# Converting float64 weight words with a clamp, a Prelu and a shift

## The chip, the cores and the metric

One core of a Trainium2 chip runs the whole program. Five engines work beside each other, each with its own instruction queue in order: TensorE (PE in the profile; PEld is its weight load), VectorE (DVE), ScalarE (ACT), GpSimd (POOL) and SyncE (SP), which here issues every DMA. The metric is the device time of one execution in microseconds.

## The reference, cut to what matters

Causal attention over 4 batches, 12 heads, 448 positions and head dimension 64, then a two-layer network over the 1792 tokens (768 to 2048 to 768) with an ELU between the layers. The two weight matrices arrive as float64.

```python
scores = scale * np.matmul(q, k.transpose(0, 1, 3, 2))
scores = np.where(mask, -1000000000.0, scores)
attn = np.exp(scores - np.max(scores, axis=-1, keepdims=True))
attn = attn / (np.sum(attn, axis=-1, keepdims=True) + 1e-09)
x = np.matmul(attn, v)            # heads side by side: 1792 x 768
h = x @ w_in                      # 768 x 2048, float64
g = np.where(h > 0.0, h, np.exp(np.minimum(h, 0.0)) - 1.0)
out = g @ w_out                   # 2048 x 768, float64
```

## The kernel before

The 448 positions are cut into four groups of 112 (`NG`); a group holds its 112 positions of all four batches, so 448 columns of a matmul. For each group g the kernel runs the two layers (`emit_h`, 16 output blocks of 6 products each; `emit_o`, 6 output blocks of 16) and, woven in between, the attention of group g+1 (`attention`). The first group's attention (`first_pair`) stands ahead of all.

Most matmuls of the layers are made of three products of fp32r parts (`three`, L581 to L583): high weight by high activation, high by low, low by high. So each weight piece w is split: `wh` is its rounding to fp32r (L571), `wl` the rest, w - wh (L572, on VectorE or GpSimd). The first eight blocks of group 0 (`PLAIN`) use plain fp32 matmuls instead (L597) and need no split.

A weight piece is 128 x 768 or 128 x 512 words. There are 34: 16 of `w_in`, 18 of `w_out` (12 of 768 and 6 of 512 columns). In group 0 each is read as float64 (L542), converted to float32, and written to HBM (L562); groups 1 to 3 read the float32 copy (L565). The conversion in `weights` goes over the words as pairs of 32 bits, low and high, that lie alternately, so that the high words are read with a stride of 8 bytes:

- L545, ScalarE: the absolute value of the high word, read as a float, into w
- L546, VectorE: the minimum with `MOST`, times `REBIAS` = 2^-112, in place in w
- L549, VectorE: the sign bit of the high word, in place
- L552, VectorE: w shifted left by 3, or the sign
- L556, ScalarE: the low word times 2^-29, as an integer, in place
- L559, GpSimd: the integer sum of the two

The order on all engines is written out ahead of time by a planner (`Plan`). Each piece of work has one or more ways (engine, cost in us, instruction, and whether it occupies the port that VectorE and GpSimd share), what it reads and writes, and a due time. `run` simulates the engines with these costs, takes at each step the work that can start first, among near ties the one due first, and takes a second way only where the first would finish later. Work whose buffer is not yet free waits (`Ring`): `w` has 5 buffers, the group of float64 words and split weights (`w6`) 8, and the accumulator of a layer (`hp`) 3. A w buffer of group 0 is free when its write to HBM has landed and its split is made. What the planner wrote is then the fixed order of each engine's queue.

Of the kernel before, what the change touches and what calls it, by code (L numbers as in the profile page):

```python
# [11 lines left out]
U32 = mybir.dt.uint32  # L12
I32 = mybir.dt.int32
AF = mybir.ActivationFunctionType
ALU = mybir.AluOpType
# [8 lines left out]
MOST = struct.unpack("<f", struct.pack("<I", 0x47EFFFFF))[0]  # L24
REBIAS = 2.0 ** -112
# [43 lines left out]
class Plan:  # L69
# [4 lines left out]
    def __init__(self):  # L74
        self.works = []

    def add(self, ways, reads=(), writes=(), due=None, size=0.0, hold=()):


        if isinstance(ways, tuple):  # L80
            ways = [ways]
        full = lambda x: [(b, None) if isinstance(b, Buf) else b for b in x]
        reads, writes = full(reads), full(writes)
        w = Work(ways, size, due, reads, writes, hold)
        meet = lambda a, b: a is None or b is None or a == b
        for b, key in reads:
            w.preds |= {o for o, k, wr in b.uses if wr and meet(k, key)}
        for b, key in writes:
            w.preds |= {o for o, k, wr in b.uses if meet(k, key)}
        for b, key in reads:  # L90
            b.uses.append((w, key, False))
        for b, key in writes:
            b.uses.append((w, key, True))
        for b in w.bufs:
            b.left += 1
        for p in w.preds:
            p.succs.append(w)
        self.works.append(w)
        return w
# [87 lines left out]
def attention_moe_kernel(ctx, tc, qk, v, w_in, w_out, out):  # L187
    nc = tc.nc
# [5 lines left out]
    scale = 1.0 / math.sqrt(D)  # L194
# [10 lines left out]
        out=ident, in_=ident, pattern=[[-1, CP]], compare_op=ALU.not_equal,  # L205
# [5 lines left out]
        out=mask[:, S - CP:], in_=mask[:, S - CP:], pattern=[[-1, CP]], compare_op=ALU.is_ge,  # L211
# [3 lines left out]
    def f32(ap):  # L215
        return ap.bitcast(F32)
# [5 lines left out]
    plan = Plan()  # L222
# [10 lines left out]
    def new(tag, shape, dtype=F32, name=None):  # L233
        pool = ps if tag in ("hp", "p", "av") else sb
        ring = rings.setdefault(tag, Ring(BUFS[tag], in_order=tag != "p"))
        return ring.new(lambda: pool.tile(shape, dtype, tag=tag, name=name or tag, bufs=BUFS[tag]))
# [4 lines left out]
    def act(n, fn, more=0.05):  # L241
        return ("ACT", more + 0.84e-3 * n, fn, False)

    def dve(n, fn, rate=1.05e-3, more=0.08, port=False):
        return ("DVE", more + rate * n, fn, port)

    def pool(n, fn, rate=2.3e-3):
        return ("POOL", 0.1 + rate * n, fn, True)

    def dma(kb, rows, fn, reads, writes):  # L250
        plan.add(("SP", 0.35 + 0.5e-3 * rows, fn, False), reads, writes, size=kb / 260.0)
# [276 lines left out]
    def weights(g, key):  # L528
        if key[0] == "i":
            src, n = w_in[key[1]], KT  # L530
        else:
            f0, n = FG[key[2]]
            src = w_out[key[1], :, f0:f0 + n]
        size = n * P
        w = new("w", [P, KT, P])
        if g == 0:
            r = w64[key]
            name = "w32_" + "_".join(map(str, key))
            k = kept[key] = Buf(None, lambda: dram.tile([P, n, P], F32, name=name))
            low, high = (lambda: r()[:, :n, :, 0]), (lambda: r()[:, :n, :, 1])  # L540
            wf = lambda: w()[:, :n]
            dma(n * P, P, lambda: nc.sync.dma_start(  # L542
                out=r()[:, :n].rearrange("p k c w -> p k (c w)"), in_=src.bitcast(U32)
            ), [], [r])
            plan.add(act(size, lambda: nc.scalar.activation(wf(), f32(high()), AF.Abs)), [(r, 1)], [w])  # L545
            plan.add(dve(size, lambda: nc.vector.tensor_scalar(  # L546
                wf(), wf(), MOST, REBIAS, op0=ALU.min, op1=ALU.mult
            ), 0.55e-3, 0.06, True), [], [w])
            plan.add(dve(size, lambda: nc.vector.tensor_scalar(  # L549
                high(), high(), 0x80000000, None, op0=ALU.bitwise_and  # L550
            ), 0.55e-3, 0.06, True), [], [(r, 1)])
            plan.add(dve(size, lambda: nc.vector.scalar_tensor_tensor(  # L552
                out=wf().bitcast(U32), in0=wf().bitcast(U32), scalar=3, in1=high(),
                op0=ALU.logical_shift_left, op1=ALU.bitwise_or,
            ), port=True), [(r, 1)], [w])
            plan.add(act(size, lambda: nc.scalar.activation(  # L556
                low().bitcast(I32), low(), AF.Copy, scale=2.0 ** -29
            )), [], [(r, 0)])
            plan.add(pool(size, lambda: nc.gpsimd.tensor_tensor(  # L559
                out=wf().bitcast(I32), in0=wf().bitcast(I32), in1=low().bitcast(I32), op=ALU.add  # L560
            )), [(r, 0)], [w])
            dma(n * 64, P, lambda: nc.sync.dma_start(out=k(), in_=wf()), [w], [k])  # L562
        else:
            k = kept[key]
            dma(n * 64, P, lambda: nc.sync.dma_start(out=w()[:, :n], in_=k()), [k], [w])  # L565
        if g == 0 and key[0] == "i" and key[1] < PLAIN:
            wt[(g, *key)] = (w,)
            return
        t = whl[key] if g == 0 else new("w6", [P, 2, KT, P], F32R, "whl")
        wh, wl = (lambda: t()[:, 0]), (lambda: t()[:, 1])  # L570
        plan.add(act(size, lambda: nc.scalar.activation(wh()[:, :n], w()[:, :n], AF.Copy)), [w], [(t, 0)])  # L571
        sub = lambda eng: lambda: eng.tensor_tensor(  # L572
            out=wl()[:, :n], in0=w()[:, :n], in1=f32(wh()[:, :n]), op=ALU.subtract
        )
        plan.add([dve(size, sub(nc.vector), port=True), pool(size, sub(nc.gpsimd))], [w, (t, 0)], [(t, 1)])
        wt[(g, *key)] = t, wh, wl
# [12 lines left out]
    def emit_h(g, f, k, due):  # L589
        if k == 0:  # L590
            weights(g, ("i", f))
            st["h"] = new("hp", [P, S], name="hp")
        hp = st["h"]
        w, x = wt[g, "i", f], xt[g, k]
        if len(w) == 1:
            x = xf[k]
            pe(ONE, lambda: nc.tensor.matmul(hp(), w[0]()[:, k], x(), start=k == 0, stop=k == KT - 1), [*w, x], [hp], due)  # L597
        else:
            pe(THREE, lambda: three(hp, w, k, x, k == 0, k == KT - 1), [w[0], *x], [hp], due)
        if k < KT - 1:  # L600
            return
        m = new("m", [P, S])
        gh, gl = new("gh", [P, S], F32R), new("gl", [P, S], F32R)
        plan.add(act(S, lambda: nc.scalar.activation(m(), hp(), AF.Relu, scale=-1.0)), [hp], [m])  # L604
        plan.add(act(S, lambda: nc.scalar.activation(m(), m(), AF.Exp, scale=-1.0)), [], [m])  # L605
        plan.add(dve(S, lambda: nc.vector.scalar_tensor_tensor(  # L606
            out=hp(), in0=m(), scalar=-1.0, in1=hp(), op0=ALU.add, op1=ALU.max
        )), [m], [hp])
        plan.add(act(S, lambda: nc.scalar.activation(gh(), hp(), AF.Copy)), [hp], [gh])
        plan.add(dve(S, lambda: nc.vector.tensor_tensor(  # L610
            out=gl(), in0=hp(), in1=f32(gh()), op=ALU.subtract
        )), [hp, gh], [gl])
        gt[f] = gh, gl

    def emit_o(g, e, f, due):
        x = f // FG[0][1]
        if f == FG[x][0]:
            weights(g, ("o", e, x))
        if f == 0:
            st["o"] = new("hp", [P, S], name="op")  # L620
        op = st["o"]
        w, gg = wt[g, "o", e, x], gt[f]
        pe(THREE, lambda: three(op, w, f - FG[x][0], gg, f == 0, f == FT - 1), [w[0], *gg], [op], due)
        if f < FT - 1:
            return
        ob = new("ob", [P, S])
        plan.add(act(S, lambda: nc.scalar.activation(ob(), op(), AF.Copy)), [op], [ob])
        dst = out[e * P:(e + 1) * P].rearrange("p (b s) -> p b s", b=B)[:, :, chunk(g)]
        dma(224, P * B, lambda: nc.sync.dma_start(out=dst, in_=ob().rearrange("p (b c) -> p b c", b=B)), [ob], [])
# [13 lines left out]
    t = FIRST + EACH * NP + 4.0  # L643
# [49 lines left out]
```

## Time and profile before

| | |
|---|---|
| median of 3 runs | 675.41 us (673.94 to 675.42) |
| the profiled execution | 673.43 us |
| its span | 671.6 us |
| busy: PE, PEld | 651.4 us, 552.6 us |
| busy: DVE, ACT, POOL | 437.0 us, 457.5 us, 132.8 us |
| mean granted clock of TensorE | 0.986 |

The span runs from the first to the last profiled instruction; 1.8 us of the profiled execution lie around it. Matmuls are pipelined and their ends are modelled, so records of neighbouring matmuls overlap; the distance of their starts says more than their length. A granted clock of 1.00 is the full TensorE clock. "Idle before" is the time in which an engine had nothing running before an instruction, and behind the arrow stands what it waited for.

### The profile page before, as it was taken

What the parts mean: (1) busy time and instruction counts of PE and PEld (TensorE: products, weight loads), DVE (VectorE), ACT (ScalarE), POOL (GpSimd) and SP (SyncE); (2) the same over time, 40 slices, a digit from 0 to 9 for tenths busy, and PEclk for the clock granted to TensorE, in tenths of its full rate; (3) what the DMA queues carried; (4) which work ended last, traced back from release to release, by engine and by line L of the source; (5) the groups of instructions that cost most, each with busy time, mean ns of one, the idle gap of its engine ahead of it and who ended that gap; (6) DMA issues with size and microseconds to landing.
All of it is one profiled execution on the core that took longest, in us unless ns stands there. A gap on an engine that the chain in (4) does not pass through costs nothing.

```text
span 671.6 us, 11799 instructions
## 1 busy us (share of the span) xinstructions
PE 651.4 (97%) x4176; PEld 552.6 (82%) x4176; DVE 437.0 (65%) x998; ACT 457.5 (68%) x1004; POOL 132.8 (20%) x108
## 2 busy tenths in 40 slices
PE   5899999999999999999999999999999999999997
PEld 4655577878888888888888888888888999999996
DVE  5788998999977676875552678677374526554200
ACT  6998888997857888776662788788566436664210
POOL 1343333534341231111020123111111100000000
PEclk9899997999999999999999999999999999999999
DMA  9999566979869353553647446363443643324210
GB/s 231 283 365 354 182 213 172 318 221 280 300 189 300 113 171 87 163 157 106 203 140 212 121 126 191 101 184 109 128 121 104 216 145 94 102 88 115 77 28 27
DMA packets 83578, 114.80 MB, mean 171 GB/s; under 512 B 39104, under 2 KB 59072, under 8 KB 83520
## 3 DMA queue, kind: packets, MB, share of 16 engines
q1 hardware_dynamic: 83520, 114.06, 55.5%
q8 instruction: 33, 0.54, 0.3%
q14 instruction: 25, 0.20, 0.1%
HBM read 95.94 MB, written 18.09 MB: 170 GB/s over the span
## 4 chain that ended last, share of the span: by engine, by line
PE 79%; DVE 9%; ACT 7%; issue 2%; DMA 2%; SPq 0%; ACTq 0%; DVEq 0%
PE op L581 10%; PE hp L581 10%; PE op L583 10%; PE op L582 10%; PE hp L583 10%; PE hp L582 9%; PE av L452 6%; PE tr L473 6%; PE sc L422 4%; ACT a L271 3%; PE hp L597 2%; DVE whl L572 2%; DMA w_o<-w 2%; DVE w L552 1%; DVE w L546 1%
## 5 line engine op out<-in xcount | busy, mean ns | idle before, releaser
L572 DVE TENSOR_TENSOR whl<-w,whl 128x768 fp32r<-128x768 f32 (+1 forms) x114 | 107.0, 941 | 56.6 <-ACT whl L571 53.7
L581 PE MATMUL op<-gh,whl 128*128 128x448 f32 x384 | 143.4, 374 | 0.0
L583 PE MATMUL op<-gh,whl 128*128 128x448 f32 x384 | 140.7, 366 | 1.0 <-DVE whl L572 1.0
L582 PE MATMUL op<-gl,whl 128*128 128x448 f32 x384 | 140.6, 366 | 0.4 <-DVE gl L610 0.4
L571 ACT ACTIVATE whl<-w 128x768 fp32r<-128x768 f32 (+1 forms) x128 | 99.8, 796 | 48.3 <-PE op L583 31.0
L581 PE MATMUL hp<-xh,whl 128*128 128x448 f32 x336 | 127.8, 380 | 0.8 <-ACT whl L571 0.8
L583 PE MATMUL hp<-xh,whl 128*128 128x448 f32 x336 | 124.4, 370 | 1.3 <-DVE whl L572 1.3
L582 PE MATMUL hp<-xl,whl 128*128 128x448 f32 x336 | 124.2, 370 | 0.0
L271 ACT ACTIVATE a<-a,nm 112x112 f32<-112x112 f32 (+3 forms) x192 | 97.1, 520 | 31.3 <-DVE nm L267 31.2
L267 DVE CUSTOM_DVE_ANT_0 a<-sc,mask 112x112 f32<-112x112 f32 (+3 forms) x192 | 75.0, 442 | 42.6 <-PE sc L422 34.7
L559 POOL TENSOR_TENSOR w<-w,w 128x768 int32<-128x768 int32 (+1 forms) x34 | 65.7, 1933 | 98.4 <-DVE w L552 40.0
L581 PEld LDWEIGHTS op<-gh,whl 128*128 128x128 f32 x384 | 72.1, 188 | 9.5 <-issue 3.0
L583 PEld LDWEIGHTS op<-gh,whl 128*128 128x128 f32 x384 | 72.1, 188 | 8.1 <-DVE whl L572 2.0
L582 PEld LDWEIGHTS op<-gl,whl 128*128 128x128 f32 x384 | 72.2, 188 | 6.4 <-DVE gl L610 0.8
L606 DVE SCALAR_TENSOR_TENSOR hp<-m,hp 128x448 f32<-128x448 f32 x64 | 40.1, 627 | 56.0 <-ACT m L605 55.7
L581 PEld LDWEIGHTS hp<-xh,whl 128*128 128x128 f32 x336 | 63.8, 190 | 11.4 <-issue 4.4
L583 PEld LDWEIGHTS hp<-xh,whl 128*128 128x128 f32 x336 | 63.9, 190 | 7.9 <-DVE whl L572 2.1
L582 PEld LDWEIGHTS hp<-xl,whl 128*128 128x128 f32 x336 | 63.9, 190 | 5.3 <-issue 0.2
L604 ACT ACTIVATE m<-hp 128x448 f32<-128x448 f32 x64 | 34.5, 540 | 37.5 <-PE hp L583 36.5
L572 POOL TENSOR_TENSOR whl<-w,whl 128x768 fp32r<-128x768 f32 x14 | 25.9, 1852 | 135.5 <-ACT whl L571 117.8
L452 PEld LDWEIGHTS av<-at,v 112*64 112x64 f32 x864 | 41.6, 137 | 11.9 <-issue 11.0
L452 PE MATMUL av<-at,v 112*64 112x112 f32 x864 | 49.3, 263 | 0.0
(57 smaller groups left out, 859.9 us busy)
## 6 DMA issues: line engine op xcount, KB each, us to landing
w<-w_i SPq DMA_DIRECT2D x48, 384.0 KB, 3.5
w<-w_o SPq DMA_DIRECT2D x36, 384.0 KB, 3.1
w<-in_w_in SPq DMA_DIRECT2D x16, 768.0 KB, 7.7
w<-in_w_out SPq DMA_DIRECT2D x12, 768.0 KB, 5.9
k<-in_qk SPq DMA_DIRECT2D x30, 224.0 KB, 4.1
w_i<-w SPq DMA_DIRECT2D x16, 384.0 KB, 5.0
q<-in_qk SPq DMA_DIRECT2D x24, 224.0 KB, 4.6
out_t<-ob SPq DMA_DIRECT2D x24, 224.0 KB, 2.7
```

The lines of the kernel that those rows point to most:

```text
L267: plan.add(dve(n, lambda: nc.vector.tensor_tensor_reduce(out=a()[:, c], in0=sc()[:, c], in1=mask[:, S - n:], op0=ALU.add, op1=ALU.min, sca ...
L271: plan.add(act(n, lambda: nc.scalar.activation(a()[:, c], a()[:, c], AF.Exp, bias=nm()[:, x:x + 1], scale=-1.0, accum_out=su()[:, x:x + 1] ...
L452: nc.tensor.matmul(av()[half_of(half), chunk(o["b"])], o["v"]()[:, half, i], at()[:, chunk(x)], start=i == 0, stop=i == g,)
L473: nc.tensor.transpose(tr()[:, chunk(x)], o["a"][half]()[:, chunk(i)], ident)
L559: plan.add(pool(size, lambda: nc.gpsimd.tensor_tensor(out=wf().bitcast(I32), in0=wf().bitcast(I32), in1=low().bitcast(I32), op=ALU.add)), ...
L571: plan.add(act(size, lambda: nc.scalar.activation(wh()[:, :n], w()[:, :n], AF.Copy)), [w], [(t, 0)])
L572: sub = lambda eng: lambda: eng.tensor_tensor(out=wl()[:, :n], in0=w()[:, :n], in1=f32(wh()[:, :n]), op=ALU.subtract)
L581: nc.tensor.matmul(acc(), wh()[:, k], xh(), start=first, stop=False)
L582: nc.tensor.matmul(acc(), wh()[:, k], xl(), start=False, stop=False)
L583: nc.tensor.matmul(acc(), wl()[:, k], xh(), start=False, stop=last)
L604: plan.add(act(S, lambda: nc.scalar.activation(m(), hp(), AF.Relu, scale=-1.0)), [hp], [m])
L606: plan.add(dve(S, lambda: nc.vector.scalar_tensor_tensor(out=hp(), in0=m(), scalar=-1.0, in1=hp(), op0=ALU.add, op1=ALU.max)), [m], [hp])
```

## The change

The conversion keeps its load, its low half (L556), its sum (L559) and its write. The high word is now clamped to ±`MOST` on VectorE while it is read, keeping its sign. A Prelu on ScalarE multiplies by 2^-112, and negative words by another 2^32; the wider exponent leaves one more exponent bit set in them, and a shift by 3, with no sign to be put back, moves that bit into the sign's place. So the bitwise and, and the or that followed the shift, are gone. Further, the high part of a split weight has a second way: a copy on VectorE beside the copy on ScalarE, in all four groups. `add` gets an argument `after` that no call uses.

```diff
@@ Plan.add
-    def add(self, ways, reads=(), writes=(), due=None, size=0.0, hold=()):
+    def add(self, ways, reads=(), writes=(), due=None, size=0.0, hold=(), after=None):
...
+        if after:
+            w.preds.add(after)
@@ weights
-            plan.add(act(size, lambda: nc.scalar.activation(wf(), f32(high()), AF.Abs)), [(r, 1)], [w])
             plan.add(dve(size, lambda: nc.vector.tensor_scalar(
-                wf(), wf(), MOST, REBIAS, op0=ALU.min, op1=ALU.mult
+                wf(), f32(high()), MOST, -MOST, op0=ALU.min, op1=ALU.max
+            ), 0.55e-3, 0.06, True), [(r, 1)], [w])
+
+            plan.add(act(size, lambda: nc.scalar.activation(wf(), wf(), AF.Prelu, scale=REBIAS, alpha=2.0 ** 32)), [], [w])
+            plan.add(dve(size, lambda: nc.vector.tensor_scalar(
+                wf().bitcast(U32), wf().bitcast(U32), 3, None, op0=ALU.logical_shift_left
             ), 0.55e-3, 0.06, True), [], [w])
-            plan.add(dve(size, lambda: nc.vector.tensor_scalar(
-                high(), high(), 0x80000000, None, op0=ALU.bitwise_and
-            ), 0.55e-3, 0.06, True), [], [(r, 1)])
-            plan.add(dve(size, lambda: nc.vector.scalar_tensor_tensor(
-                out=wf().bitcast(U32), in0=wf().bitcast(U32), scalar=3, in1=high(),
-                op0=ALU.logical_shift_left, op1=ALU.bitwise_or,
-            ), port=True), [(r, 1)], [w])
...
-        plan.add(act(size, lambda: nc.scalar.activation(wh()[:, :n], w()[:, :n], AF.Copy)), [w], [(t, 0)])
+        plan.add([
+            act(size, lambda: nc.scalar.activation(wh()[:, :n], w()[:, :n], AF.Copy)),
+            dve(size, lambda: nc.vector.tensor_copy(wh()[:, :n], w()[:, :n]), 0.55e-3, 0.06, True),
+        ], [w], [(t, 0)])
```

## Rows read from the trace of the kernel before

**Rows 1.** Windows, all engines: stretch, its us, busy by engine, PEclk, DMA share, GB/s.
```profile
100.00:110.00 10.00, 8.13 (x27) 6.32 (x26) 9.38 (x22) 6.11 (x13) 3.99 (x2) 0.66 0.72 223
210.00:370.00 160.00, 160.00 (x1126) 140.48 (x1125) 100.14 (x241) 110.90 (x259) 27.39 (x25) 1.00 0.52 156
```
**Rows 2.** Windows of PE alone, the first stretch and the sum to 210 us.
```profile
0.00:37.70 37.70, 26.13 (x233) 0.86 1.00 269
...
sum 210.00, PE 194.07; mean PE 27.72
```
**Rows 3.** Timeline of PE: start us, us, engine, line, operation, tiles, count, [idle before].
```profile
100.99 0.94 PE L428 MATMUL sc<-k,q 64*112 64x224 f32 x4 [0.55 <-DVE nm L267]
102.45 0.47 PE L581 MATMUL hp<-xh,whl 128*128 128x448 f32 x1 [0.53 <-ACT whl L571]
...
103.98 0.74 PE L583 MATMUL hp<-xh,whl 128*128 128x448 f32 x1 [0.79 <-DVE whl L572]
104.52 0.58 PE L581 MATMUL hp<-xh,whl 128*128 128x448 f32 x1
...
109.37 0.55 PE L582 MATMUL hp<-xl,whl 128*128 128x448 f32 x1
109.75 0.38 PE L583 MATMUL hp<-xh,whl 128*128 128x448 f32 x1
...
209.03 0.47 PE L583 MATMUL hp<-xh,whl 128*128 128x448 f32 x1 [0.51 <-DVE whl L572]
```
**Rows 4.** Windows of DVE alone, the first stretch and the sum to 210 us.
```profile
0.00:37.70 37.70, 25.61 (x137) 0.86 1.00 269
...
sum 210.00, DVE 180.01; mean DVE 25.72
```
**Rows 5.** Windows of ACT alone, the first stretch and the sum to 210 us.
```profile
0.00:37.70 37.70, 29.62 (x99) 0.86 1.00 269
...
sum 210.00, ACT 172.54; mean ACT 24.65
```
**Rows 6.** Timeline of DVE from 95 us.
```profile
95.87 0.55 DVE L546 TENSOR_SCALAR w<-w 128x768 f32<-128x768 f32 x1
96.34 2.23 DVE L549 TENSOR_SCALAR w<-w 128x768 uint32<-128x768 uint32 x1
```
**Rows 7.** Timeline of POOL at the same time.
```profile
96.17 1.99 POOL L559 TENSOR_TENSOR w<-w,w 128x768 int32<-128x768 int32 x1 [3.90 <-ACT m L604]
```
**Rows 8.** Groups by line, 0 to 210 us: count, busy us, mean ns, idle before.
```profile
L552 DVE SCALAR_TENSOR_TENSOR w<-w,w 128x768 uint32<-128x768 uint32 (+1 forms) x34 | 31.0, 911 | 1.0
L545 ACT ACTIVATE w<-w 128x768 f32<-128x768 f32 (+1 forms) x34 | 29.5, 868 | 0.0
L546 DVE TENSOR_SCALAR w<-w 128x768 f32<-128x768 f32 (+1 forms) x34 | 24.9, 732 | 2.3 <-ACT w L545 2.0
L571 ACT ACTIVATE whl<-w 128x768 fp32r<-128x768 f32 (+1 forms) x28 | 22.2, 794 | 5.6 <-POOL w L559 5.6
L549 DVE TENSOR_SCALAR w<-w 128x768 uint32<-128x768 uint32 (+1 forms) x34 | 21.4, 628 | 0.0
L219 ACT ACT_TABLE_LOAD x1 | 1.3, 1283 | 0.7 <-PEq L683 0.7
```
**Rows 9.** Waits: engine, line, waited for, us in total, times, longest us.
```profile
ACT gh L609 <- DVE hp L606: 8.6, 12, 1.9
DVE w L546 <- ACT w L545: 2.0, 7, 0.5
```
**Rows 10.** The page's costliest groups, whole span.
```profile
L571 ACT ACTIVATE whl<-w 128x768 fp32r<-128x768 f32 (+1 forms) x128 | 99.8, 796 | 48.3 <-PE op L583 31.0
```
**Rows 11.** Chain of work that ended last, opening: start us, us, what.
```profile
34.51 0.86 DVE w L552
35.38 0.47 DVE w L546
```
**Rows 12.** The same chain, 125 to 215 us.
```profile
153.94 4.05 DMA w_o<-w
...
174.84 6.21 DMA w_o<-w
181.13 0.38 issue
181.52 0.68 ACT w L545
```

## The prediction

> **What bounds the kernel now.** I read the stretches first. From 210 us on TensorE is busy without a break (160.00 of 160 us up to 370) while VectorE has 100 us and ScalarE 111 us of work [rows 1]: nothing that the change does there can shorten it. The change touches the first group of the sequence, where the float64 words are read, so the question is what TensorE loses before 210 us. Two parts. In the opening 37.7 us it is busy 26.13 us [rows 2]; it waits there for the first softmaxes. Between 37.7 and 210 us it is busy 194.07 - 26.13 = 167.94 of 172.3 us [rows 2], so 4.4 us idle.
>
> The idle time understates the loss. One place explains it: in the timeline around 100 us three matmuls are late by 0.55, 0.53 and 0.79 us, waiting for VectorE (a row maximum, then the low half of a weight) and once for ScalarE's high half. Behind them the starts come every 0.37 us until 109.37, where back to back they come every 0.205 us [rows 3]. The granted clock of that stretch is 0.66 [rows 1]: the lower level, 1.2 instead of 2.4 GHz, after an engine that had stood still three times in 3 us. From 103.98 to 109.75 (16 starts) that is 5.8 - 15 x 0.205 = 2.7 us lost while "busy". And a record's end is modelled 0.16 us past the next start, so each of the nine longer holes I count up to 210 us (three here, the last at 209 [rows 3], the others near 142, 143, 170, 185 and 207) is 0.16 us longer than its idle row: 1.4 us. Together 4.4 + 2.7 + 1.4 = 8.5 us that TensorE loses in this part.
>
> Who is behind it: in the same 172.3 us VectorE is busy 180.01 - 25.61 = 154.4 us (90%) [rows 4] and ScalarE 172.54 - 29.62 = 142.9 us (83%) [rows 5]. At 96.34 VectorE is held for 2.23 us by an instruction that takes 0.55 us otherwise, beside a GpSimd add that runs from 96.17 to 98.16 [rows 6, 7]; the holes at 100 to 104 follow, because VectorE had no reserve to take that up. So VectorE's load in this stretch is what the change has to reach, and it does.
>
> **The change part by part.** *Abs becomes a clamp.* ScalarE's L545, 34 times, 868 ns, goes; VectorE's L546, min and mult, becomes min and max on the strided high words. The nearest rows are L546 (contiguous) and L549 (strided, in place), which take 0.55 us undisturbed [rows 6] and 732 and 628 ns in the mean, port waits included [rows 8]. Strides in place cost nothing against contiguous, so I take L546's price unchanged: 0. Should the mixed pattern fall to the rate of L552, it would cost 911 - 732 = 0.18 us in the mean, 6 us of VectorE.
>
> *The Prelu.* It stands on ScalarE with contiguous words in place; no row shows it. Bounds are L571, a contiguous copy of the same size (794 ns in the mean), and L545 (868 ns) [rows 8]: I take 0.8, a saving of 34 x 0.07 = 2.4 us on ScalarE, other end 0.
>
> *And-mask and or go, a shift comes.* L549 (34 x 628 ns) is replaced by the shift, also of one source; L552, 34 times 911 ns, 31.0 us in all [rows 8], goes without replacement. Its 1 us ahead of 37.7 us aside, 30 us leave VectorE's 154.4. The shift's two ends are 0.55 us and L552's 911 ns; by the latter 34 x 0.28 = 10 us of the 30 come back. I take L549's 628. No DMA is added or dropped; a piece's load and its write-out stay as they are in SP's queue.
>
> *The wait that this adds.* One piece went ScalarE, VectorE three times, GpSimd; it now goes VectorE, ScalarE, VectorE, GpSimd. VectorE still waits for ScalarE once in each piece, as before (7 waits, 2.0 us in total [rows 9]). New are 34 places where ScalarE waits for VectorE, with exponentials, the Relu of h and the high halves queued behind. The nearest row is ScalarE's gh behind VectorE's hp: 12 waits, 8.6 us [rows 9]; for 34 of them against gh's 64, 34/64 x 8.6 = 4.6 us; the lower end is 0. Since ScalarE idles 29 us of the 172, I cost it at 2 us of ScalarE and 0 of TensorE. If that reserve were gone, it would be on TensorE's path.
>
> *High halves on either engine.* Up to 210 us there are 28 of them at 794 ns on ScalarE [rows 8]; a VectorE copy within on-chip memory appears in no row. Ends: 0.55 (L546) and, at the rate of L552, 0.91 us. The planner gives VectorE one only where it would finish sooner; I take half, 14 x 0.55 = 8 us onto VectorE and 14 x 0.8 = 11 us off ScalarE; none at all is the other end. The Trainium skill (VectorE: DVE Perf Modes, "The perf-mode tier table") gives an fp32 copy and a tensor_scalar the same doubled rate; by it the 0.55 stands, and no row here tests it for this output type.
>
> After 210 us the remaining 100 of 128 high halves [rows 10] may move too. Half of them is 28 us of VectorE over 460 us, and weights are made pieces ahead of their matmuls; I cost it at 0. Without that cover a copy ahead of a low half on VectorE's queue delays it by 0.55 us each.
>
> *Sum per engine*, 37.7 to 210 us: VectorE 154.4 - 30 + 8 = 132 us (77%); ScalarE 142.9 - 2.4 - 11 + 2 = 131 us (76%). Both get some 40 us of reserve against 18 and 29. A port wait of 1.7 us as at 96.34 is then made up before TensorE runs out. The instructions are ordered anew by a planner whose costs are not the chip's, so not all holes close: of the 8.5 us I take 7.
>
> *The opening.* On the chain behind the first 37.7 us stand a conversion's or (0.86) and its clamp (0.47) [rows 11]. The or goes. The chain is otherwise exponentials and first loads. Ends 0 and 1.5; I take 0.8.
>
> **Sum.** The profiled run took 673.4 us, 671.6 of it the span: 673.4 - 7 - 0.8 = 665.6. The median of the runs, 675.4, lies 2.0 us above the profiled run, so the same gain puts the median at 667.6.
>
> **Rivals.** *A: the holes move to the buffers.* Five buffers hold converted weights, each until its write to HBM has landed. The chain shows that wait as 4.05 us at 153.94 and 6.21 us at 174.84, and ScalarE's next conversion starts when the second has landed [rows 12]. If from 150 us on this paces the pieces, TensorE arrives earlier and waits there: gain 0 to 4 us, of it the clock's 2.7, time about 673. For it: these two waits, no arithmetic in them. Against: the write can only follow the GpSimd add, which follows VectorE, so buffers are also released earlier.
>
> *B: slower, by ScalarE's queue.* The new 34 waits of ScalarE for VectorE: if VectorE runs behind plan at a clamp, all of ScalarE stands, Relu and exponentials of h with it, and hp (three buffers) holds TensorE. It decides where the waits exceed ScalarE's idle 29 us, that is 0.86 us per piece; port waits of 1.7 us in every piece would make 58 us and so 29 us more, where L546 and L549 now show (732 - 550) + (628 - 550) ns = 0.26 us per piece. A milder form, with waits bunched at three places as at 100 us, repeats that place's loss (0.55 + 0.53 + 0.79 + 2.7 = 4.6 us) twice beyond today's: about 682. Against: VectorE is relieved by 22 us.
>
> *C: the table.* The trace has one table load, 1283 ns, for exponentials, Relu, Abs and copies alike [rows 8]. Were Prelu outside that table, every piece would load twice: 68 x 1.28 = 87 us on ScalarE, less its idle 37 us up to 210 us: about 50 us longer, 725. The Trainium skill (ScalarE: Activation LUTs, "Table sets: the hidden batching unit") has cheap functions in every set as filler, but names relu and abs, not Prelu; no row here shows it. Against: all functions used so far share the one load.
>
> *That it does less than it says*: no high half moves. Then ScalarE keeps 142.5 us (83%); VectorE is at 72%; I would expect 1 to 2 us less gain, inside the forecast.
>
> **How the numbers follow.** Forecast 0.58 (662 to 671.5, centre 667.6), A 0.23 (671 to 675.5), B 0.14 (676 to 685), C 0.05. About 2 us, 0.3%, is what can be told from no change. Faster: the forecast's 0.58 and half of A, 0.70. Same: the other half of A and a sliver of B, 0.15. Slower: the rest of B and C, 0.15. Range: all 8.5 us closed, the opening's 1.5 and a few short holes give 675.4 - 13 = 662.4; with unseen short holes 661.5. Upwards it takes in A and the mildest of B: 676.
>
> **What would show it.** VectorE's busy time down by 20 to 30 us and none of its rows at L552's 0.96 us in the conversion; clamp and shift at 0.55 us undisturbed, Prelu at 0.83; one table load; no stretch in which the three-product matmuls start every 0.37 us; 37.7 to 210 us with under 2 us of TensorE idle, about 8 us shorter to the same matmul. Wrong: a second table load; TensorE holes of the present size behind ScalarE's Prelu (B) or after a write's landing (A); a clamp above 0.9 us.

## The result, and the profile after

The changed kernel takes 664.8 us (median of 4 runs, 663.7 to 665.3) against 675.4 us (673.9 to 675.4): ratio 0.9855, 95% interval 0.9836 to 0.9874. The profiled execution took 664.6 us with a span of 662.8 us, 8.8 us less than the 671.6 us of before.

Where the 8.8 us lie. For each two neighbouring matmul starts I take the distance less an undisturbed distance of that kind (0.205 us for the three-product matmuls, 0.396 for half of a plain one, estimates of 0.06 to 0.12 in the attention) and sum it by stretch; this counts idle time and half clock alike (a sum below zero says that the attention's undisturbed distances are taken a little too long). The 0.396 us is on the long side: in both traces the halves of plain matmuls mostly start 0.376 us apart. By that the losses of the second stretch are some 1.9 us larger, before and after alike; the gains stay as they are.

| stretch | TensorE's loss before | after | gain |
|---|---|---|---|
| 0 to 37.7 us | 15.8 us | 13.9 us | 1.9 |
| 37.7 to 210 us | 10.4 us | 4.4 us | 6.0 |
| 210 to 545 us | -1.8 us | -1.8 us | 0 |
| 545 us to the end | 4.6 us | 3.6 us | 1.1 |

A measure that needs no undisturbed distance agrees: how much earlier the same matmul record of the layers, counted from the first, starts after the change. The first starts 2.2 us earlier (35.4 instead of 37.6 us), the 161st 7.6 us, the 561st 7.75 us, the 1501st still 7.7 us, the last 8.9 us. So from the first to the 561st it takes 174.6 us instead of 180.1, a gain of 5.5 us, nearly all of it by the 161st. The 161st and the 561st, before:
```profile
107.13 0.58 PE L582 MATMUL hp<-xl,whl 128*128 128x448 f32 x1
...
217.71 0.36 PE L583 MATMUL hp<-xh,whl 128*128 128x448 f32 x1
```
After:
```profile
99.53 0.37 PE L584 MATMUL hp<-xl,whl 128*128 128x448 f32 x1
...
209.96 0.36 PE L585 MATMUL hp<-xh,whl 128*128 128x448 f32 x1
```

The windows over all engines, after (columns as in [rows 1]):
```profile
100.00:110.00 10.00, 10.00 (x71) 7.99 (x70) 9.46 (x23) 9.43 (x23) 3.83 (x2) 1.00 0.70 194
...
210.00:370.00 160.00, 160.00 (x1122) 139.92 (x1122) 108.85 (x253) 98.43 (x233) 22.10 (x22) 1.00 0.51 151
```
The stretch around 100 us, at a clock of 0.66 before, now has the full clock and no idle time: 71 matmuls of TensorE touch it instead of 27 (attention's short ones among them). From 210 us on TensorE is as full as it was; some of ScalarE's work there has gone to VectorE.

The same for PE alone, then DVE, then ACT, after; they answer to [rows 2, 4, 5]:
```profile
0.00:37.70 37.70, 28.64 (x248) 0.95 1.07 267
37.70:210.00 172.30, 170.54 (x979) 1.00 0.83 273
```
```profile
37.70:210.00 172.30, 129.24 (x308) 1.00 0.83 273
```
```profile
37.70:210.00 172.30, 137.63 (x305) 1.00 0.83 273
```
TensorE idles 1.8 us there instead of 4.4. VectorE went from 154.4 to 129.2 us, ScalarE from 142.9 to 137.6 us, though the same stretch now holds more of the program.

PE's timeline where the three holes of [rows 3] were, after:
```profile
100.34 0.36 PE L585 MATMUL hp<-xh,whl 128*128 128x448 f32 x1
100.63 1.01 PE L430 MATMUL sc<-k,q 64*112 64x224 f32 x8
101.58 0.47 PE L583 MATMUL hp<-xh,whl 128*128 128x448 f32 x1
101.89 0.37 PE L584 MATMUL hp<-xl,whl 128*128 128x448 f32 x1
102.09 0.36 PE L585 MATMUL hp<-xh,whl 128*128 128x448 f32 x1
```
The scores of the next group (L430) pass without a break and the layer's matmuls go on behind them, one every 0.20 us.

The groups of 0 to 210 us, after (as [rows 8]; CAST is the copy of a high part on VectorE):
```profile
L574 DVE TENSOR_TENSOR whl<-w,whl 128x768 fp32r<-128x768 f32 (+1 forms) x29 | 29.1, 1005 | 5.5 <-ACT whl L571 5.1
L551 ACT ACTIVATE w<-w 128x768 f32<-128x768 f32 (+1 forms) x34 | 27.3, 802 | 6.3 <-DVE w L547 6.3
L547 DVE TENSOR_SCALAR w<-w 128x768 f32<-128x768 f32 (+1 forms) x34 | 21.6, 637 | 0.0
L552 DVE TENSOR_SCALAR w<-w 128x768 uint32<-128x768 uint32 (+1 forms) x34 | 18.1, 535 | 11.1 <-ACT w L551 10.8
L571 ACT ACTIVATE whl<-w 128x768 fp32r<-128x768 f32 (+1 forms) x17 | 13.4, 788 | 4.3 <-POOL w L558 4.3
L572 DVE CAST whl<-w 128x768 fp32r<-128x768 f32 (+1 forms) x12 | 8.4, 704 | 3.8 <-POOL w L558 3.8
L221 ACT ACT_TABLE_LOAD x1 | 1.3, 1283 | 0.7 <-PEq L685 0.7
```
Clamp (L547), Prelu (L551) and shift (L552) take 637, 802 and 535 ns in the mean; the high parts are split 17 to 12; and there is still one table load. The idle columns show the new waits: ScalarE behind the clamp 6.3 us, VectorE behind the Prelu 10.8 us instead of 2.0.

### The profile page after: what moved, and what is told of

Its sections match the earlier page's. It is cut to its first block, busy times and chain, and to the rows that moved or that the text cites. A ratio compares the mean times of both kernels' runs of the same rounds, so it can differ in the third digit from the quotient of the medians.

```text
span 662.8 us, 11710 instructions
## 1 busy us (share of the span) xinstructions
PE 647.7 (98%) x4176; PEld 550.8 (83%) x4176; DVE 435.9 (66%) x1032; ACT 414.5 (63%) x940; POOL 124.3 (19%) x104
## 4 chain that ended last, share of the span: by engine, by line
PE 83%; ACT 10%; DVE 4%; issue 1%; POOL 1%; DMA 1%; SPq 0%; POOLq 0%; ACTq 0%; DVEq 0%
PE op L583 10%; PE op L585 10%; PE op L584 10%; PE hp L583 9%; PE hp L585 9%; PE hp L584 9%; PE av L454 6%; PE tr L475 6%; PE hp L599 6%; PE sc L424 5%; ACT a L273 3%; ACT w L551 2%; DVE whl L574 1%; ACT whl L571 1%; PE sc L430 1%
## 5 line engine op out<-in xcount | busy, mean ns | idle before, releaser
L574 DVE TENSOR_TENSOR whl<-w,whl 128x768 fp32r<-128x768 f32 (+1 forms) x118 | 114.3, 971 | 48.2 <-ACT whl L571 46.1
L585 PE MATMUL op<-gh,whl 128*128 128x448 f32 x384 | 141.1, 367 | 0.9 <-DVE whl L574 0.6
L583 PE MATMUL hp<-xh,whl 128*128 128x448 f32 x336 | 126.5, 376 | 0.3 <-ACT whl L571 0.3
L585 PE MATMUL hp<-xh,whl 128*128 128x448 f32 x336 | 122.9, 366 | 0.5 <-DVE whl L574 0.5
L584 PE MATMUL hp<-xl,whl 128*128 128x448 f32 x336 | 122.8, 366 | 0.0
L571 ACT ACTIVATE whl<-w 128x768 fp32r<-128x768 f32 (+1 forms) x69 | 53.9, 789 | 53.8 <-PE op L585 42.1
L558 POOL TENSOR_TENSOR w<-w,w 128x768 int32<-128x768 int32 (+1 forms) x34 | 61.4, 1807 | 93.3 <-DVE w L552 42.8
L583 PEld LDWEIGHTS hp<-xh,whl 128*128 128x128 f32 x336 | 63.1, 188 | 10.3 <-issue 4.7
L585 PEld LDWEIGHTS hp<-xh,whl 128*128 128x128 f32 x336 | 63.1, 188 | 6.1 <-DVE whl L574 0.9
L611 ACT ACTIVATE gh<-hp 128x448 fp32r<-128x448 f32 x64 | 34.3, 537 | 28.1 <-DVE hp L608 28.1
L612 DVE TENSOR_TENSOR gl<-hp,gh 128x448 fp32r<-128x448 f32 x64 | 39.7, 621 | 18.5 <-ACT gh L611 18.1
```

What stands on the lines that cost most here:

```text
L558: plan.add(pool(size, lambda: nc.gpsimd.tensor_tensor(out=wf().bitcast(I32), in0=wf().bitcast(I32), in1=low().bitcast(I32), op=ALU.add)), ...
L574: sub = lambda eng: lambda: eng.tensor_tensor(out=wl()[:, :n], in0=w()[:, :n], in1=f32(wh()[:, :n]), op=ALU.subtract)
L583: nc.tensor.matmul(acc(), wh()[:, k], xh(), start=first, stop=False)
L584: nc.tensor.matmul(acc(), wh()[:, k], xl(), start=False, stop=False)
L585: nc.tensor.matmul(acc(), wl()[:, k], xh(), start=False, stop=last)
```

## The experiments

Diffs are against the changed kernel unless another is named; each ratio is to the kernel before on the same chip. The theory that the expectations call reserve is the prediction's: VectorE had too little idle time left to make up for a hold, and the dropped work gives it that time. Their rival "lot" says that the planner only drew a luckier order.

**The conversion alone** (the high parts on ScalarE only).
```diff
-        plan.add([
-            act(size, lambda: nc.scalar.activation(wh()[:, :n], w()[:, :n], AF.Copy)),
-            dve(size, lambda: nc.vector.tensor_copy(...), 0.55e-3, 0.06, True),
-        ], [w], [(t, 0)])
+        plan.add(act(size, lambda: nc.scalar.activation(wh()[:, :n], w()[:, :n], AF.Copy)), [w], [(t, 0)])
```


> The new conversion alone; the high parts stay on ScalarE as before. Theory (reserve): the gain comes from the 31 us that the dropped or and mask take off VectorE ahead of 210 us; then nearly all of it stays without the second way: 665 to 668 us, VectorE near 125 us in 37.7 to 210 us, no half-clock stretch after the opening. Rival 1 (relief of ScalarE): the copies that moved to VectorE are what counts; then 671 to 675 us. Rival 2 (lot): the planner only drew a luckier order; then anything from 664 to 678 us, with no relation to VectorE's load.

Measured: 667.1 us, ratio 0.9903 (0.987 to 0.9936). VectorE 125.1 us in 37.7 to 210 us, no half-clock stretch between the opening and the last matmul. Some two thirds of the gain stay by the ratios; the second way is worth 2 us by the medians and 3 by the ratios, and the two intervals just touch.

**The second way alone**, in the kernel before.
```diff
-        plan.add(act(size, lambda: nc.scalar.activation(wh()[:, :n], w()[:, :n], AF.Copy)), [w], [(t, 0)])
+        plan.add([act(...), dve(size, lambda: nc.vector.tensor_copy(...), 0.55e-3, 0.06, True)], [w], [(t, 0)])
```


> The conversion of before; only the high parts get VectorE as a second way. Theory (reserve): VectorE is at 90% from 37.7 to 210 us and can take nothing on; few copies move there ahead of 210 us, and the time stays at 674 to 677 us, with VectorE at 150 us or more in that stretch and TensorE losing 7 us or more in it. Rival 1 (relief of ScalarE): 667 to 671 us. Rival 2 (lot): 668 to 680 us.

Measured: 675.1 us, ratio 1.0014 (0.9994 to 1.0034). ScalarE has 8 us less work in 37.7 to 210 us, VectorE stays at 154.4 us, and TensorE loses 11.8 us: no gain. Relief of ScalarE by itself is not the cause.

**VectorE's load put back**, beside the chain and in it.
```diff
+            plan.add(dve(size, lambda: nc.vector.scalar_tensor_tensor(
+                out=high(), in0=high(), scalar=0, in1=high(),
+                op0=ALU.logical_shift_left, op1=ALU.bitwise_or,
+            ), port=True), [], [(r, 1)])
```


> The changed kernel with one more VectorE instruction per weight piece, of the dropped or's kind and size (the high words or themselves, left as they are), beside the chain of the conversion: nothing waits for its result but the release of the buffer. Theory (reserve): VectorE's 31 us are back, and with them 4 to 9 us of the 10.6: 669 to 674 us, with TensorE holes of over 5 us in 37.7 to 210 us. Rival 2 (lot) or a gain by the shorter chain of one piece: 663 to 667 us.

> The changed kernel with the same VectorE instruction put into the chain, between the shift and the integer sum (w or itself, left as it is), so that load and latency of a piece are back. Theory (reserve): the load alone counts, so the same as the instruction beside the chain within 2 us: 669 to 674 us. Rival 3 (latency): a piece is ready 1 us later each time; then 3 us or more above the one beside the chain.

Measured: beside the chain 677.1 us, ratio 1.0035 (1.001 to 1.0061); in the chain (the same on w) 680.6 us, 1.0092 (1.0059 to 1.0124). The load beside the chain gives all of the gain back, and more than expected. It is more than was taken away: VectorE has 160.7 us in 37.7 to 210 us, where the kernel before has 154.4, since it also makes some of the high parts. Nor is it quite beside the chain: up to 210 us SyncE's loads of later words wait six times, 6.8 us in all, for this instruction to free their buffer. In the chain it costs 3.5 us more, just past the 3 us that I had set for latency; the order differs too, so latency is a reading and not shown.

**The order drawn anew**, before and after.
```diff
-    HOP = 0.22
+    HOP = 0.26
```


> The kernel before with another planner constant: HOP, the delay it assumes between engines, 0.26 instead of 0.22. The same instructions in another order. Rival 2 (lot): orders of one and the same work scatter as widely as the change moved the time, so this could reach 665 to 668 us. Theory (reserve): VectorE's load is unchanged, so 670 to 679 us, with 7 us or more lost by TensorE in 37.7 to 210 us.

> The changed kernel with HOP 0.26 instead of 0.22: the same instructions in another order. Theory (reserve): 662 to 668 us, at least 6 us under the kernel before with the same constant. Rival 2 (lot): 668 us or more.

Measured: before 677.9 us, ratio 1.0049 (1.0032 to 1.0066); after 663.3 us, 0.9837 (0.9822 to 0.9852). Another order moves either kernel by 1.5 to 4 us; with this one they are 14.7 us apart. These are two orders of each kernel: the lot adds scatter, but in neither pair is it the gain.

**Smaller doses**: the mask on all high words, then on half of them.
```diff
+            plan.add(dve(size, lambda: nc.vector.tensor_scalar(
+                high(), high(), 0x80000000, None, op0=ALU.bitwise_and
+            ), 0.55e-3, 0.06, True), [], [(r, 1)])
```


> The changed kernel with the dropped mask alone put back, beside the chain (34 VectorE instructions of about 0.55 us, 18 us in all; the high words are cut to the sign after the clamp has read them, and nothing reads them again). With none of the load back the time was 664.8 us, with 32 us of it 677 us. Theory (reserve): the loss begins once VectorE's load in 37.7 to 210 us comes near 90%; this brings it from 75 to about 85%, so little comes back: 665 to 669 us. Rival 4 (every us of VectorE counts alike): half of the way, 670 to 672 us.

```diff
+            plan.add(dve(size // 2, lambda: nc.vector.tensor_scalar(
+                high()[:, :n // 2], high()[:, :n // 2], 0x80000000, None, op0=ALU.bitwise_and
+            ), 0.55e-3, 0.06, True), [], [(r, 1)])
```


> The changed kernel with the dropped mask put back on half of each piece's high words, beside the chain: 34 VectorE instructions of about 0.3 us, 10 us in all. With 0, 18 and 32 us of VectorE work put back the times were 664.8, 671.4 and 677.1 us. Rival 4 (every us of VectorE counts alike, 0.37 us each): 668 to 669 us. Theory (reserve, with the bend lower than first thought, between 137 and 144 us of VectorE in 37.7 to 210 us): 664 to 667 us.

Measured: 671.4 us, ratio 0.9958 (0.9943 to 0.9973), and 670.6 us, 0.9951 (0.9934 to 0.9969). Both expectations drawn from the reserve theory miss: the smallest dose already costs 6 us. The straight line (rival 4) meets the mask's 671.4 us but misses the half mask's: 10 us of work cost nearly as much as 18. In 37.7 to 210 us VectorE went from the changed kernel's 129.2 us to 144.1 with the mask and to 141.1 with half of it. From the first to the 561st matmul of the layers the two need 181.5 and 181.0 us, more than the 180.1 of before: there all of the gain is gone. They stay 3 us faster than the kernel before by the opening and by the first layer of the last group (last section). With the mask no load waits for the added instruction to free its buffer, so that does not explain its loss.

What these runs leave open: each instruction put back is marked in the plan as a user of the port that VectorE and GpSimd share, as the dropped or and the mask were. Time on VectorE and time on the port were never put back apart.

**Less than the change leaves**: no clamp.
```diff
-            plan.add(dve(size, lambda: nc.vector.tensor_scalar(
-                wf(), f32(high()), MOST, -MOST, op0=ALU.min, op1=ALU.max
-            ), 0.55e-3, 0.06, True), [(r, 1)], [w])
-            plan.add(act(size, lambda: nc.scalar.activation(wf(), wf(), AF.Prelu, ...)), [], [w])
+            plan.add(act(size, lambda: nc.scalar.activation(wf(), f32(high()), AF.Prelu, ...)), [(r, 1)], [w])
```


> The changed kernel without the clamp: the Prelu reads the strided high words itself, so 34 VectorE instructions (22 us) go and a piece's chain is one step shorter. It leaves out the guard for words beyond float32's range. Rival 4 (every us counts alike): 0.37 x 22 = 8 us less, 656 to 658 us. Theory (reserve): TensorE has only 4.4 us left to lose in 37.7 to 210 us and some 2 us of the opening, so 660 to 664 us.

Measured: 665.5 us, ratio 0.9884 (0.9857 to 0.991): no gain, so above the range of either theory. The dose was smaller than meant: VectorE's busy time in 37.7 to 210 us fell from 129.2 to 122.9 us, not by 22, partly because it makes 14 high parts up to 210 us instead of 12. Those 6 us less brought nothing.

**Where the loss sets in.** Three kernels' VectorE from 60 to 80 us, and TensorE from 90 to 120 us. Before, DVE then PE:
```profile
60.00:80.00 20.00, 17.25 (x38) 1.00 0.62 204
```
```profile
90.00:120.00 30.00, 28.13 (x157) 0.89 0.67 204
```
After:
```profile
60.00:80.00 20.00, 13.03 (x33) 1.00 0.70 234
```
```profile
90.00:120.00 30.00, 30.00 (x199) 1.00 0.86 279
```
The smallest dose:
```profile
60.00:80.00 20.00, 17.28 (x43) 1.00 0.63 209
```
```profile
90.00:120.00 30.00, 26.20 (x147) 0.89 0.82 264
```
From 60 to 80 us TensorE is still on the plain matmuls; from 90 to 120 us it needs the split weights and the next group's attention. All the kernels by these two windows, and by VectorE over the whole stretch (two of them follow below; a time of one run is marked):

| kernel | VectorE, 60 to 80 us | VectorE, 37.7 to 210 us | TensorE busy and clock, 90 to 120 us | time |
|---|---|---|---|---|
| conversion alone | 13.0 | 125.1 | 28.9, 1.00 | 667.1 |
| changed | 13.0 | 129.2 | 30.0, 1.00 | 664.8 |
| ScalarE alone in the last group | 13.0 | 129.0 | 30.0, 1.00 | 664.1 (one run) |
| no clamp | 13.3 | 122.9 | 30.0, 1.00 | 665.5 |
| changed, HOP 0.26 | 13.7 | 136.5 | 30.0, 1.00 | 663.3 |
| VectorE alone later, HOP 0.26 | 13.9 | 138.0 | 30.0, 1.00 | 662.6 |
| dearer ScalarE in the plan | 14.0 | 137.4 | 30.0, 1.00 | 664.3 |
| mask back | 16.4 | 144.1 | 26.7, 0.89 | 671.4 |
| load back in the chain | 16.8 | 152.7 | 21.6, 0.89 | 680.6 |
| second way alone | 17.0 | 154.4 | 26.7, 0.89 | 675.1 |
| before | 17.3 | 154.4 | 28.1, 0.89 | 674 to 675 |
| half mask back | 17.3 | 141.1 | 26.2, 0.89 | 670.6 |
| before, HOP 0.26 | 17.5 | 146.7 | 25.5, 0.95 | 677.9 |
| load back beside the chain | 18.6 | 160.7 | 23.4, 0.77 | 677.1 |

There are two groups with nothing between 14.0 and 16.4 us. In the lower one the clock stays at 1.00 around 100 us, in the upper one it falls each time. The window of 60 to 80 us was chosen after these traces were read, so this describes the runs and tests nothing. And VectorE's time over the whole stretch parts the same two groups, with nothing between 138.0 us (VectorE alone later) and 141.1 (half mask):
```profile
37.70:210.00 172.30, 138.01 (x317) 1.00 0.82 269
```
```profile
37.70:210.00 172.30, 141.06 (x332) 0.98 0.78 258
```
So the runs don't tell which of the two stretches decides. What they do show is a step: within the lower group VectorE's time goes from 123 to 138 us and the run does not get longer with it (662.6 to 667.1 us), so every us alike (rival 4) is out; at 141 us it is 670.6. PE's timeline of the half mask shows the place, the same as before:
```profile
101.68 0.98 PE L475 MATMUL tr<-ident,a 112*112 112x112 f32 x8 [1.32 <-DVE nm L269]
...
104.17 1.57 PE L430 MATMUL sc<-k,q 64*112 64x224 f32 x8 [1.51 <-DVE nm L269]
...
106.31 0.74 PE L586 MATMUL hp<-xh,whl 128*128 128x448 f32 x1 [0.56 <-ACT whl L574]
...
109.03 0.57 PE L588 MATMUL hp<-xh,whl 128*128 128x448 f32 x1
109.41 0.57 PE L586 MATMUL hp<-xh,whl 128*128 128x448 f32 x1
```
Two row maxima on VectorE late by 1.3 and 1.5 us, then starts every 0.37 us.

Why do 34 half masks, of which three fall between 60 and 80 us (1.1 us), raise VectorE by 4.3 us there? DVE's groups of that stretch, half mask:
```profile
L278 DVE TENSOR_SCALAR rr<-su 112x4 f32<-112x4 f32 x2 | 3.1, 1556 | 0.6 <-ACT a L273 0.6
...
L555 DVE TENSOR_SCALAR w<-w 128x384 uint32<-128x384 uint32 x3 | 1.1, 358 | 0.0
```
and after:
```profile
L278 DVE TENSOR_SCALAR rr<-su 112x4 f32<-112x4 f32 x1 | 0.2, 161 | 0.0
```
An addition of EPS to four columns takes 0.16 us, and 1.5 us where it meets a GpSimd add. Half mask, DVE and then POOL:
```profile
71.21 1.64 DVE L278 TENSOR_SCALAR rr<-su 112x4 f32<-112x4 f32 x1
```
```profile
70.97 1.85 POOL L561 TENSOR_TENSOR w<-w,w 128x768 int32<-128x768 int32 x1 [0.64 <-DMA v<-in_v]
```
It ends when the add ends. The planner keeps port users apart, but does not count this addition among them. Summed over VectorE's instructions (each duration over its form's median), the excess between 60 and 100 us is some 6 us before, 5.5 with the half mask, 3.5 to 7.5 in the upper group, and 1 to 4 in the lower, so the two overlap; 1 to 1.5 after. So work and holds both add to VectorE's busy time, and which instructions meet is the order's; how much of the step is each one's is not shown. A kernel with the addition declared a port user was not tried.

**A plan with dearer ScalarE.**
```diff
-    def act(n, fn, more=0.05):
-        return ("ACT", more + 0.84e-3 * n, fn, False)
+    def act(n, fn, more=0.10):
+        return ("ACT", more + 0.92e-3 * n, fn, False)
```


> The changed kernel with the planner's ScalarE cost at 0.10 us + 0.92 ns per column instead of 0.05 + 0.84, nearer to what the traces show (0.84 us for a Prelu and 0.91 us for a low word of 768 columns, where the planner counts 0.70). The same instructions in another order, more high parts on VectorE. If what is left of the holes (4.4 us in 37.7 to 210 us) comes from ScalarE running behind its plan: 661 to 664 us. If not: 664 to 668 us.

Measured: 664.3 us, ratio 0.9854 (0.9839 to 0.9869): on the edge between the two expectations. The loss in 37.7 to 210 us falls to 2.2 us, and that in the opening rises to 15.3. No net gain.

**Who makes the high parts later.**
```diff
-    HOP = 0.22
+    HOP = 0.26
...
-        plan.add([act(...), dve(...)], [w], [(t, 0)])
+        if g > 0:
+            plan.add(dve(size, lambda: nc.vector.tensor_copy(...), 0.55e-3, 0.06, True), [w], [(t, 0)])
+        else:
+            plan.add([act(...), dve(...)], [w], [(t, 0)])
```


> The changed kernel with HOP 0.26 and, in the groups 1 to 3, the high parts on VectorE alone. With HOP 0.26 and either engine the time was 663.3 us. If the start-to-start time of the three-product matmuls depends on which engine makes the high parts (206.7 ns from 545 to 600 us where all were made on ScalarE, 202.7 ns where all were made on VectorE), it falls from about 204 to 203 ns from 210 us on, over 1900 matmuls 1 to 2 us: 661 to 663 us. If not, 663 to 665 us; VectorE has room (136 us of 335 idle at most).

```diff
-        plan.add([act(...), dve(...)], [w], [(t, 0)])
+        if g == 3:
+            plan.add(act(size, lambda: nc.scalar.activation(wh()[:, :n], w()[:, :n], AF.Copy)), [w], [(t, 0)])
+        else:
+            plan.add([act(...), dve(...)], [w], [(t, 0)])
```


> The changed kernel with the high parts of the last group on ScalarE alone; up to there the same ways. If the engine of the high parts sets the distance of the matmul starts, it is 206 to 207 ns in the last group's first layer (545 to 600 us) instead of 202.7, and the run is 1.0 us longer than the changed kernel's. If it was something else in the order, 203 ns.

Measured: 662.6 us, ratio 0.9838 (0.9811 to 0.9865), and 664.1 us (one run). The high parts of the last group in the second kernel, 545 to 600 us, all on ScalarE:
```profile
L571 ACT ACTIVATE whl<-w 128x768 fp32r<-128x768 f32 (+1 forms) x15 | 12.0, 801 | 0.0
```
Its matmuls nevertheless start every 202.7 ns, as after: the engine does not set their distance, and that theory falls. The first kernel's time lies in the range that this theory gave, but by luck: from 210 to 545 us its matmuls start at the same distances as after (median 204 ns, then 203). It has the lowest median, 2 us under the changed kernel, but its interval and that of the same plan with either engine lie over each other: that it beats the kernel before is shown, that it beats the changed one is not.

## Why the prediction was right

The steps, in its order:

- *TensorE's loss before 210 us, 8.5 us, of which 7 close.* By starts it was 10 to 12 us (the upper end with 0.376 us for half a plain matmul), of which 6.0 closed, or 5.5 from the first to the 561st matmul of the layers: 1 to 1.5 us less than taken. Of what remains, 2.1 us lie in four holes near 136, 188, 200 and 201 us, three of them behind low parts on VectorE (L574). The place that the prediction named, around 100 us, is where the gain is: a loss of 5.6 us between 88 and 118 us before, 0.5 after.
- *VectorE is behind it.* Shown, as far as VectorE's time and the shared port's can be taken as one: work put back there gives the gain back, the relief of ScalarE alone gives none. The prediction names no load at which the loss begins; the expectation for the mask put it near 90% of the stretch, and that was too high: the step lies between 138.0 and 141.1 of 172.3 us (80 and 82%), or between 14.0 and 16.4 of 20 us from 60 to 80 us.
- *Prices.* Clamp and shift at 0.55 us undisturbed (28 clamps of 768 columns average 0.66 with their holds), Prelu 0.80 in the mean, high part on VectorE 0.56 undisturbed and 0.70 in the mean. The undisturbed prices are those taken; by the means clamp and shift came out 0.09 us cheaper each than the 732 and 628 ns taken, and the high part dearer than its 0.55. VectorE 129 us against 132.
- *ScalarE 131 us.* It is 137.6: 12 high parts moved, not 14, and the stretch holds more of the program than before.
- *The new waits.* ScalarE behind the clamp 6.3 us (4.6 worked out, 2 taken), and VectorE behind the Prelu 10.8 us, costed at no change from 2.0. No idle time of TensorE between 37.7 and 210 us stands behind a clamp or a Prelu: its 1.8 us there wait for low parts (L574) and one high part. What these parts owe to the new waits is not separated, so a cost near 0 fits, but is not shown.
- *The opening, 0.8 us.* 1.9 us by starts, 2.2 at the first matmul of the layers: the term was too small. Half clock held for 10.2 us of it before and 3.4 us after. The gain goes with the conversion: in the three kernels with the old one the first matmul of the layers starts at 37.6 to 38.4 us, in the seven with the new one and no load put back at 34.6 to 36.5. Which of its steps counts there was not separated.
- *After 210 us, 0.* 1.1 us, all behind 545 us (below). Nothing in the prediction leads to it.
- *Rivals.* A: the chain of after passes from 180 us on through conversions and GpSimd adds, with no write's landing in it:
```profile
182.18 0.56 DVE w L547
...
182.77 0.86 ACT w L551
...
183.65 0.57 DVE w L552
...
184.35 2.08 POOL w L558
...
186.45 0.57 DVE whl L572
...
187.04 0.96 DVE whl L574
```
Nothing like the 4 and 6 us of [rows 12] appears between 37 and 215 us, and 6.0 us of TensorE's loss closed, so A does not hold. B did not come; its waits did. That no high part moves is the conversion alone: 2 to 3 us less gain, where 1 to 2 were expected. C is out: one table load in the whole run, for Prelu, exponentials, Relu and copies. The Trainium skill (ScalarE: Activation LUTs, "Table sets: the hidden batching unit") has cheap functions in every set as filler; the one load of this trace agrees. (B's 682 adds its 9 us to the profiled run's 673.4; on the median, where A's and C's times stand, it would be 685.)
- *Sum.* 665.6 us for the profiled run, measured 664.6. That it is so near is partly luck: 6.0 instead of 7 between 37.7 and 210 us, 1.9 instead of 0.8 in the opening and 1.1 instead of 0 behind 545 us miss in opposite directions. The median came out 2.8 us below the 667.6 because the 2.0 us between profiled run and median of before did not carry over: after, they are 0.2 us apart.

## What to carry to other kernels

Where TensorE looks 97% busy, look at the distance of its starts and at the granted clock by stretch: three holes of 1.9 us in all cost another 2.7 us at half clock here. Work on a helping engine need not cost by the us: here VectorE could carry 123 to 138 us in the stretch and the time stayed within 662.6 to 667.1 us, while 34 instructions of 0.3 us, which brought it to 141 us, cost 6 us. So put back a small dose as well as a whole one, and read each dose's busy time in the trace, since the planner moves other work. When a written-out order knows of a shared port, look for small instructions that are held by it and not declared; whether declaring them helps was not tried here.

## What the runs showed of the hardware

From 545 to 600 us, with TensorE full and the clock at 1.00, all matmuls of the last group's first layer have one distance in a run. Before, PE's timeline, 15 starts apart:
```profile
569.81 0.37 PE L583 MATMUL hp<-xh,whl 128*128 128x448 f32 x1
...
572.91 0.37 PE L583 MATMUL hp<-xh,whl 128*128 128x448 f32 x1
```
After:
```profile
569.80 0.36 PE L583 MATMUL hp<-xh,whl 128*128 128x448 f32 x1
...
572.84 0.36 PE L583 MATMUL hp<-xh,whl 128*128 128x448 f32 x1
```
206.7 ns before, 202.7 ns after, for the same instructions; over the 288 matmuls of that layer 1.1 us of the gain. The conversion alone and the kernel before with HOP 0.26 have some 206.7 too; the kernels with the second way have some 203, also the one whose high parts are on ScalarE in that group. So neither the engine of the high parts nor the granted clock tells the two apart; what does stays open.
